# Fifteen-product groups: temporaries' sums moved between engines, weight splits and normalisation steps at other places

## The chip, the cores and the metric

The kernel runs on one core of a Trainium2 chip. The core has five engines that run side by side, each through its own queue in order: TensorE (PE in the profile; its weight loads are PEld), VectorE (DVE), ScalarE (ACT), GpSimd (POOL) and SyncE (SP), which here issues the DMAs. The metric is the device time of one execution in microseconds (us). Three runs of the kernel before took 1329.54, 1331.19 and 1333.52 us; the median is 1331.19 us.

## The reference

All arrays are float32. A pooled attention (2 batches, 8 heads, 1152 keys) gives 1152 tokens of 512 features. They go through a dense layer pair with the Mish function, and the result x through eight experts whose weights per token come from eight rounds of Sinkhorn normalisation:

```python
def _moe2_ref(x, w_gate, w1, w2):            # x 1152x512, w1 8x512x1024, w2 8x1024x512
    logits = x @ w_gate
    P = np.exp(logits - logits.max())
    for _ in range(8):
        P /= P.sum(1, keepdims=True) + 1e-09
        P /= P.sum(0, keepdims=True) + 1e-09
        P *= N / E
    out = 0
    for e in range(E):
        h = np.maximum(x @ w1[e], 0.0)
        out += P[:, e:e + 1] * (h @ w2[e])
    return out
```

Attention and Mish layers are untouched by the change; the experts are where it acts.

## The kernel before

**Arithmetic.** Every float32 operand is kept as two fp32r parts, high and low (`split_hi`, `split_lo`, lines 74 to 81). A product is three matmuls: high by low, low by high, high by high.

**The experts.** The 64 hidden chunks (8 experts by 8 chunks of 128) are worked through in order. The first four go the plain way (`expert_up`, and `down(-1, t)`), the other 60 in 20 groups of three (`groups`, g = 0 to 19). A group first computes its hidden values, 3 chunks by 3 token blocks of 384. Plainly that would be 9 block pairs by 2 halves of the features, 18 products; the kernel uses a scheme with 15 products of sums of blocks (`ORDER3`): sums of weights (`w_sum`), split into high and low (`w_split`), sums of tokens made once before (`x_prep`), and sums of the results afterwards (`after`). The program names a product by its number (9, 13, 3, 11, 12, 1, 2, 5, 10, 14, 7, 8, 0, 6, 4, in this order) and a result block by chunk and token block ("00" is chunk 0, token block 0). Each product is six matmuls of 384 columns (L983), so a product phase has 90.

**PSUM.** The nine result blocks of a group live in the eight PSUM banks: pool `ps_o` has three, `ps_h` five. Blocks 01, 10 and 22 come from `ps_o`, the other six from `ps_h` in the order 00, 12, 11, 02, 20, 21. Block 21, which product 7 (the eleventh) opens, therefore gets the bank of block 00 and has to wait until 00 has been read for the last time.

**Results.** ACT copies some results out of PSUM (`copy`, L1000) as temporaries t9, t13, t3, t11, u12, t1, t10, u14, u7. Six sums or differences of temporaries (`pair`, L1005) follow, two on POOL (s11 = t3 - t9 and u12 = u12 - t11), four on DVE. A block is finished (`fin`) by adding a temporary to the bank on DVE (L1014), the high part by a Relu on ACT (L1018) and the low part on DVE (L1019), which is issued after the L1014 of the next block to be finished. So 00 is released by this chain on DVE, in order: add 00 (needs u12), low part of 10, add 11 (needs s11), low part of 00.

**Down.** Then `down(g, t)` for nine tiles of 128 tokens: 9 matmuls of 512 columns each (L1142) into a `ps_o` bank, 81 in all. DVE adds the result, times the gate, to `oacc` (L1150). Five of the 20 groups hold chunks of two experts: there a tile has two segments with two banks and two L1150. In group 0 the gate is applied later, as POOL scales `oacc` (L1195).

**The order** on each engine is the order of the code; nothing is reordered. During the downs of a group `next_weights` makes the next group's eleven weight sums on DVE in steps k = 0 to 2 (L949) and splits the first eight (high part ACT, low part POOL) in steps 1 to 3. The other seven are split after products 0 to 6, and the second weights of the group (`down_split`, three chunks, both parts on POOL) after products 0, 2 and 4. The raw weights go through three SBUF buffers, `wraw`: two tiles of first and two of second weights a group, so a load waits for the last reader of the tile three places earlier.

**Sinkhorn.** `gate_steps` holds ten steps: `gate_max`, `gate_exp` (with the first row normalisation) and eight `sinkhorn_cols`. A column step is a small matmul over `csum` on PE and six short DVE instructions that end in the next `csum`. A step is taken at j = 0 and 2 of the remaining `expert_up`s, after tiles 4, 6 and 8 of `down(-1)`, and after products 2, 5, 8, 11 and 14 of group 0.

Of the kernel before, what the change touches and what calls it, by code (L numbers as in the profile page):

```python
# [23 lines left out]
def pool_attention_mish_sinkhorn_kernel(  # L24
# [790 lines left out]
    def sinkhorn_cols(it):  # L815
        ps = ps_h.tile([P, 512], F32, tag="h", name=f"psk{it}")
        nc.tensor.matmul(ps[:, 0:E], lhsT=ones, rhs=csum, start=True, stop=True)
        nc.vector.reciprocal(crec, ps[:, 0:E])
        nc.vector.scalar_tensor_tensor(
            out=Pv, in0=Pv, scalar=float(NT) / E, in1=crec.unsqueeze(1).to_broadcast([P, NTT, E]),  # L820
            op0=ALU.mult, op1=ALU.mult)
        if it + 1 < ROUNDS:
            sinkhorn_rows()
# [106 lines left out]
    def down_split(g, j):  # L930
        if g not in wdt:
            wdt[g] = tuple(wpools["d0"].tile([P, 4, GF], F32R, tag="wd" + x, name=f"wdb{x}{g}") for x in "hl")
        split_hi(nc.gpsimd, wdt[g][0][:, j, :], raws_d[g][j])
        split_lo(nc.gpsimd, wdt[g][1][:, j, :], raws_d[g][j], wdt[g][0][:, j, :])
# [10 lines left out]
    def w_sum(g, k):  # L945
        n, a, op, b = WSUM[k]
        inplace = {11: "10", 0: "21"}.get(n)
        out = w_get(g, inplace) if inplace else wsum.tile([P, HD, P], F32, tag=f"s{n}", name=f"s{n}_{g}")
        nc.vector.tensor_tensor(out=out, in0=w_get(g, a), in1=w_get(g, b), op=PLUS[op])  # L949
        ws[g, n] = out  # L950
# [71 lines left out]
    def after(g, n):  # L1022

        v, o = nc.vector, nc.gpsimd
# [5 lines left out]
        if n == 3:  # L1030
            copy(g, "t3", "10")
            pair(g, o, "s11", "t3", "-", "t9")
# [3 lines left out]
        if n == 12:  # L1036
            copy(g, "u12", "11")
            pair(g, o, "u12", "u12", "-", "t11")
# [64 lines left out]
    with tc.tile_pool(name="xt", bufs=3, side="right") as xt_p:  # L1103
        todo_x = list(range(len(XSUM)))
        for j, u in enumerate(ups):
            if j in (0, 2):
                gate_step()
            expert_up(NG1, *u)
            for _ in range(2 if j % 2 else 1):
                if todo_x:  # L1110
                    x_prep(todo_x.pop(0))
# [11 lines left out]
    wdt[-1] = w2t[NG1]  # L1123

    def down(g, t):
# [101 lines left out]
```

## Time and profile before

| | |
|---|---|
| runs, median (range) | 1331.19 us (1329.54 to 1333.52) |
| profiled execution | 1332.02 us, span in the trace 1329.8 us |
| PE busy, share of the span | 1239.2 us, 93% |
| DVE | 888.2 us, 67% |
| POOL | 700.4 us, 53% |
| ACT | 623.3 us, 47% |
| mean granted TensorE clock | 0.985 |

The span falls into attention (to about 350 us), the Mish layers (to about 480 us), the change to the experts with `down(-1)` (to 539.79 us) and the 20 groups (to the end). PE is busy nearly all the time, and its order is fixed, so the places to read are those where it waits: an instruction that stalls on PE delays everything behind it. Matmuls are pipelined: one of 384 columns is shown as 0.34 us, but the next starts about 0.174 us after it. A row with `[2.68 <-DVE hlall L1019]` says that the engine stood idle 2.68 us before this instruction, until DVE finished the instruction of line 1019 that writes `hlall`.

### The profile page before, as it was taken

The page shows a single profiled execution, that of the slowest core. Times are in us where ns is not written, and L with a number is a line of the kernel's source. Part 1 is how long each engine was busy: PE and PEld are TensorE (multiplying, and loading weights), DVE is VectorE, ACT ScalarE, POOL GpSimd, SP SyncE. Part 2 cuts the span into 40 slices and gives each one's busy share as a digit, 9 for nine tenths or more (in the row PEclk, how much of TensorE's full clock was granted, in tenths as well). Part 3 has the DMA queues.
Part 4 walks back from the last instruction along what each step waited for, and adds up shares of the span by engine and source line. Part 5 has one row for each costly group of instructions (what it writes and reads, how often), then busy time and mean ns, then how long its engine had stood idle before and what let it go on. Part 6 is the DMA issues. An engine that isn't in the chain of part 4 may idle for free.

```text
span 1329.8 us, 19342 instructions
## 1 busy us (share of the span) xinstructions
PE 1239.2 (93%) x6832; PEld 1133.4 (85%) x6832; DVE 888.2 (67%) x1726; ACT 623.3 (47%) x1432; POOL 700.4 (53%) x738
## 2 busy tenths in 40 slices
PE   8999999999999997898999998998999998999898
PEld 7999999999999996787788887877887876888687
DVE  7899999955443338667666666667656677766665
ACT  7899998875544434332233332323333332333231
POOL 7888888544343324383455444445455444554442
PEclk9999999999999999899999999999999999999999
DMA  4433332222222100110111110111111011111011
GB/s 116 101 92 92 92 96 70 71 83 83 89 82 78 40 17 8 40 35 22 48 48 40 48 48 16 41 48 48 41 48 32 25 48 48 41 48 48 21 35 71
DMA packets 55759, 73.15 MB, mean 55 GB/s; under 512 B 5744, under 2 KB 37872, under 8 KB 55664
## 3 DMA queue, kind: packets, MB, share of 16 engines
q1 hardware_dynamic: 55664, 71.93, 18.9%
q8 instruction: 54, 0.88, 0.3%
q14 instruction: 41, 0.34, 0.1%
HBM read 64.50 MB, written 2.36 MB: 50 GB/s over the span
## 4 chain that ended last, share of the span: by engine, by line
PE 68%; DVE 13%; POOL 11%; issue 5%; ACT 2%; DMA 0%; POOLq 0%; DVEq 0%; SPq 0%; ACTq 0%
PE po L1142 25%; PE c L983 9%; PE ph L219 8%; PE po L725 8%; PE psS L441 6%; PE psA L520 6%; PE psT L495 5%; POOL wslotsl L81 4%; DVE c L1014 2%; DVE s L949 2%; DVE hlall L1019 2%; POOL wdbl L81 2%; POOL wdbh L78 2%; DVE oacc L1150 2%; POOL sparel L1005 1%
## 5 line engine op out<-in xcount | busy, mean ns | idle before, releaser
L81 POOL TENSOR_TENSOR wslotsl<-s,wslotsh 128x256 fp32r<-128x256 f32 x180 | 140.6, 791 | 236.2 <-ACT wslotsh L74 236.1
L1142 PE MATMUL po<-wdbl,hhall 128*128 128x512 f32 (+1 forms) x543 | 217.0, 400 | 15.9 <-DVE oacc L1150 15.5
L1150 DVE SCALAR_TENSOR_TENSOR oacc<-po,Pm,oacc 128x512 f32<-128x512 f32 (+1 forms) x217 | 159.6, 745 | 86.6 <-PE po L1142 83.5
L1142 PE MATMUL po<-wdbh,hlall 128*128 128x512 f32 (+1 forms) x543 | 214.6, 395 | 0.0
L1142 PE MATMUL po<-wdbh,hhall 128*128 128x512 f32 (+1 forms) x543 | 214.5, 395 | 0.0
L1018 ACT ACTIVATE hhall<-c 128x384 fp32r<-128x384 f32 x180 | 88.6, 492 | 180.7 <-DVE c L1014 178.0
L81 POOL TENSOR_TENSOR wslotsl<-rawu,wslotsh 128x256 fp32r<-128x256 f32 x120 | 94.0, 799 | 134.6 <-ACT wslotsh L74 134.6
L1000 ACT ACTIVATE t<-c 128x384 f32<-128x384 f32 x80 | 39.2, 490 | 264.4 <-PE c L983 264.4
L1142 PEld LDWEIGHTS po<-wdbl,hhall 128*128 128x128 f32 x543 | 102.4, 189 | 47.4 <-DVE oacc L1150 24.0
L1142 PEld LDWEIGHTS po<-wdbh,hhall 128*128 128x128 f32 x543 | 102.4, 189 | 24.5
L1142 PEld LDWEIGHTS po<-wdbh,hlall 128*128 128x128 f32 x543 | 102.5, 189 | 22.7
L501 DVE TENSOR_TENSOR etl<-psT,eth 128x384 fp32r<-128x384 f32 (+1 forms) x240 | 112.1, 504 | 9.4 <-ACT eth L498 9.3
L466 POOL TENSOR_SCALAR e<-e,rc 128x1152 f32<-128x1152 f32 x72 | 89.4, 1242 | 43.5 <-DVE rc L465 15.7
L446 DVE TENSOR_SCALAR_CACHE_REDUCE sc<-psS 128x1152 f32<-128x1152 f32 x72 | 97.4, 1353 | 14.6 <-PE psS L441 13.6
L1019 DVE SCALAR_TENSOR_TENSOR hlall<-c,hhall 128x384 fp32r<-128x384 f32 x180 | 98.3, 546 | 2.0
L983 PE MATMUL c<-x2h,wslotsl 128*128 128x384 f32 x280 | 97.5, 348 | 0.0
L498 ACT ACTIVATE eth<-psT 128x384 fp32r<-128x384 f32 (+1 forms) x240 | 92.7, 482 | 8.8 <-PE psT L495 8.7
L983 PE MATMUL c<-x2l,wslotsh 128*128 128x384 f32 x280 | 96.6, 345 | 0.0
L983 PE MATMUL c<-x2h,wslotsh 128*128 128x384 f32 x280 | 96.4, 344 | 0.0
L1014 DVE TENSOR_TENSOR c<-c,t 128x384 f32<-128x384 f32 x80 | 44.8, 560 | 74.7 <-ACT t L1000 73.2
L454 ACT ACTIVATE e<-sc,nm 128x1152 f32<-128x1152 f32 x72 | 92.1, 1279 | 0.5 <-DVE sc L446 0.5
L495 PE MATMUL psT<-ident,e 128*128 128x128 f32 x648 | 85.6, 275 | 1.3 <-POOL e L466 0.8
(349 smaller groups left out, 3261.9 us busy)
## 6 DMA issues: line engine op xcount, KB each, us to landing
rawd<-in_moe_w_dram SPq DMA_DIRECT2D x60, 256.0 KB, 2.9
rawu<-in_moe_w_dram SPq DMA_DIRECT2D x30, 384.0 KB, 3.2
raw<-in_moe_w_in_dram SPq DMA_DIRECT2D x16, 512.0 KB, 3.8
raw<-in_moe_w_out_dram SPq DMA_DIRECT2D x16, 512.0 KB, 3.7
kraw<-in_k_dram SPq DMA_DIRECT2D x16, 288.0 KB, 3.2
vraw<-in_v_dram SPq DMA_DIRECT2D x16, 288.0 KB, 2.8
qraw<-in_q_dram SPq DMA_DIRECT2D x7, 576.0 KB, 4.3
qT<-qT SPq DMA_DIRECT2D x28, 128.0 KB, 2.5
```

The costliest lines, as they stand in the source:

```text
L81: eng.tensor_tensor(out=lo, in0=src, in1=hi.bitcast(F32), op=ALU.subtract)
L219: nc.tensor.matmul(ps[:, 0:TH], lhsT=a, rhs=b, start=(n == 0), stop=(n == len(ops) - 1))
L446: nc.vector.tensor_scalar(sc, ps[:, :, 0:TH], -1.0, None, op0=ALU.mult, op1=ALU.min, accum_out=nm)
L454: nc.scalar.activation(e, sc.rearrange("p a b -> p (a b)"), AF.Exp, bias=nm, scale=-1.0, accum_out=rs)
L495: nc.tensor.transpose(ps[:, i, :], e[:, c * P:(c + 1) * P], ident)
L498: nc.scalar.activation(eh[:, cs, o:o + b - a], ps[:, 0:3, a:b], AF.Copy)
L501: nc.vector.tensor_tensor(out=el[:, cs, o:o + b - a], in0=ps[:, 0:3, a:b], in1=eh[:, cs, o:o + b - a].bitcast(F32), op=ALU.subtract)
L725: nc.tensor.matmul(ps[:, 0:TH], lhsT=a, rhs=b, start=(n == 0), stop=(n == len(ops) - 1))
L983: nc.tensor.matmul(cb[c], lhsT=a_, rhs=b_, start=FIRST[n] and m == 0, stop=LAST[n] and m == len(ops) - 1, skip_group_check=True)
L1019: los.append(lambda: nc.vector.scalar_tensor_tensor(out=lo, in0=b, scalar=0.0, in1=hi.bitcast(F32), op0=ALU.max, op1=ALU.subtract))
L1142: nc.tensor.matmul(ps[:, 0:w], lhsT=a, rhs=b[:, c, cs], start=(n == 0), stop=(n == len(ops) - 1))
L1150: nc.vector.scalar_tensor_tensor(out=oa, in0=ps[:, 0:w], scalar=gate, in1=oa, op0=ALU.mult, op1=ALU.add)
```

## The change

Nothing is computed differently but for the order of some sums. Six things move:

1. s11 and u12 are computed on DVE (`v`) in place of POOL (`o`).
2. The three second-weight splits of a group: the first in step 7 of the downs before (in group 0 after product 0), the others after products 7 and 9 (were 0, 2, 4). The tile is one ring of four chunk places for all groups.
3. The weight sums are spread over steps 0 to 6 of the downs; sums 8, 10 and 14 are made on POOL.
4. In two-expert groups the second segment's bank comes from `ps_h`; the column sums of Sinkhorn come from `ps_o`.
5. The gate steps are taken later: `expert_up` j = 2 and 4, tiles 7 and 8 of `down(-1)`, products 3 and 5 of group 0, tiles 1, 3, 5 of its downs, product 3 of group 1.
6. The scaling of `oacc` moves from group 0 to group 1: products 10, 12, 14, then the down tiles, three ahead.

```diff
-        ps = ps_h.tile([P, 512], F32, tag="h", name=f"psk{it}")
+        ps = ps_o.tile([P, 512], F32, tag="o", name=f"psk{it}")
...
     def down_split(g, j):
-        if g not in wdt:
-            wdt[g] = tuple(wpools["d0"].tile([P, 4, GF], F32R, tag="wd" + x, name=f"wdb{x}{g}") for x in "hl")
-        split_hi(nc.gpsimd, wdt[g][0][:, j, :], raws_d[g][j])
-        split_lo(nc.gpsimd, wdt[g][1][:, j, :], raws_d[g][j], wdt[g][0][:, j, :])
+        if "all" not in wdt:
+            wdt["all"] = tuple(wpools["d0"].tile([P, 4, GF], F32R, tag="wd" + x, name=f"wdb{x}") for x in "hl")
+        wh, wl = wdt[g, j] = tuple(y[:, (CH * g + j) % 4, :] for y in wdt["all"])
+        split_hi(nc.gpsimd, wh, raws_d[g][j])
+        split_lo(nc.gpsimd, wl, raws_d[g][j], wh)
...
-            pair(g, o, "s11", "t3", "-", "t9")
+            pair(g, v, "s11", "t3", "-", "t9")
...
-            pair(g, o, "u12", "u12", "-", "t11")
+            pair(g, v, "u12", "u12", "-", "t11")
...
-            if j in (0, 2):
+            if j in (2, 4):
                 gate_step()
...
-                pl, tag = (ps_h, "h") if g < 0 and 3 <= t < 8 else (ps_o, "o")
+                pl, tag = (ps_h, "h") if (3 <= t < 8 if g < 0 else si) else (ps_o, "o")
...
-        for j in {0: range(0, 4), 1: range(4, 8), 2: range(8, 11)}.get(k, ()):
-            w_sum(g, j)
+        v, o = nc.vector, nc.gpsimd
+        for n, eng in {0: ((5, v), (8, o), (11, v)), 1: ((12, v), (2, v)), 2: ((10, o), (4, v)), 3: ((14, o),),
+                       4: ((0, v),), 5: ((7, v),), 6: ((6, v),)}.get(k, ()):
+            w_sum(g, n, eng)
...
+        if k == 7 and g > 0:
+            down_split(g, 0)
+
+    def scale(k):
+        nc.gpsimd.tensor_scalar(
+            oacc[:, TILES[k], :], oacc[:, TILES[k], :], Pm[:, TILES[k], 0:1], 0.0, op0=ALU.mult, op1=ALU.add)
...
-        if t in (4, 6, 8):
+        if t in (7, 8):
             gate_step()
...
-            if k in (0, 2, 4):
-                down_split(g, k // 2)
+            if k in ((0, 7, 9) if g == 0 else (7, 9)):
+                down_split(g, {0: 0, 7: 1, 9: 2}[k])
...
-            if g == 0 and k % 3 == 2:
+            if (g, k) in ((0, 3), (0, 5), (1, 3)):
                 gate_step()
+            if g == 1 and k in (10, 12, 14):
+                assert not gate_steps
+                scale(k // 2 - 5)
...
-            if g == 0:
-                assert not gate_steps
-                nc.gpsimd.tensor_scalar(
-                    oacc[:, t, :], oacc[:, t, :], Pm[:, t, 0:1], 0.0, op0=ALU.mult, op1=ALU.add)
+            if g == 0 and k in (1, 3, 5):
+                gate_step()
+            if g == 1 and k + 3 < NTT:
+                scale(k + 3)
```

First place: DVE in the product phase of group 5 (one expert), from its first instruction to the low part of block 00. Before (L1014 finishes a block, L1019 is a low part, L1005 a sum of temporaries):

```order
L1014 TENSOR_TENSOR c_5_8347<-c_5_8347,t_5_8369 128x384
L1014 TENSOR_TENSOR c_5_8375<-c_5_8375,t_5_8396 128x384
L1019 SCALAR_TENSOR_TENSOR hlall<-c_5_8347,hhall 128x384
L1005 TENSOR_TENSOR t_5_8369<-sparel,t_5_8369 128x384
L1014 TENSOR_TENSOR c_5_8362<-c_5_8362,spareh 128x384
L1019 SCALAR_TENSOR_TENSOR hlall<-c_5_8375,hhall 128x384
L1014 TENSOR_TENSOR c_5_8403<-c_5_8403,sparel 128x384
L1019 SCALAR_TENSOR_TENSOR hlall<-c_5_8362,hhall 128x384
```

The same stretch of the changed kernel, where these lines are 1016, 1021 and 1007:

```order
L1016 TENSOR_TENSOR c_5_8341<-c_5_8341,t_5_8359 128x384
L1007 TENSOR_TENSOR sparel<-t_5_8372,t_5_8348 128x384
L1016 TENSOR_TENSOR c_5_8365<-c_5_8365,t_5_8384 128x384
L1021 SCALAR_TENSOR_TENSOR hlall<-c_5_8341,hhall 128x384
L1007 TENSOR_TENSOR spareh<-spareh,t_5_8384 128x384
L1007 TENSOR_TENSOR t_5_8359<-sparel,t_5_8359 128x384
L1016 TENSOR_TENSOR c_5_8352<-c_5_8352,spareh 128x384
L1021 SCALAR_TENSOR_TENSOR hlall<-c_5_8365,hhall 128x384
L1016 TENSOR_TENSOR c_5_8391<-c_5_8391,sparel 128x384
L1021 SCALAR_TENSOR_TENSOR hlall<-c_5_8352,hhall 128x384
```

Two sums of temporaries, `sparel` (s11) and `spareh` (u12), now stand on DVE ahead of the addition to block 00 (the sixth row before, the seventh now).

Second place: POOL in the same product phase, from the low part of split 8. `wslotsl` are low parts of first weights, `wdbh` and `wdbl` the parts of the second weights. Before:

```order
L81 TENSOR_TENSOR wslotsl<-s_5_8238,wslotsh 128x256
L78 TENSOR_SCALAR wdbh_8358<-rawd_0_8298 128x512
L81 TENSOR_TENSOR wdbl_8359<-rawd_0_8298,wdbh_8358 128x512
L81 TENSOR_TENSOR wslotsl<-s_5_8240,wslotsh 128x256
L1005 TENSOR_TENSOR sparel<-t_5_8382,t_5_8354 128x384
L81 TENSOR_TENSOR wslotsl<-s_5_8262,wslotsh 128x256
L78 TENSOR_SCALAR wdbh_8358<-rawd_0_8298 128x512
L81 TENSOR_TENSOR wdbl_8359<-rawd_0_8298,wdbh_8358 128x512
L81 TENSOR_TENSOR wslotsl<-s_5_8220,wslotsh 128x256
L1005 TENSOR_TENSOR spareh<-spareh,t_5_8396 128x384
L81 TENSOR_TENSOR wslotsl<-rawu_1_8159,wslotsh 128x256
L78 TENSOR_SCALAR wdbh_8358<-rawd_1_8301 128x512
```

After, to the end of the phase:

```order
L81 TENSOR_TENSOR wslotsl<-s_5_8247,wslotsh 128x256
L81 TENSOR_TENSOR wslotsl<-s_5_8266,wslotsh 128x256
L81 TENSOR_TENSOR wslotsl<-s_5_8302,wslotsh 128x256
L81 TENSOR_TENSOR wslotsl<-s_5_8212,wslotsh 128x256
L81 TENSOR_TENSOR wslotsl<-rawu_1_8151,wslotsh 128x256
L81 TENSOR_TENSOR wslotsl<-s_5_8315,wslotsh 128x256
L81 TENSOR_TENSOR wslotsl<-s_5_8249,wslotsh 128x256
L78 TENSOR_SCALAR wdbh<-rawd_0_8286 128x512
L81 TENSOR_TENSOR wdbl<-rawd_0_8286,wdbh 128x512
L78 TENSOR_SCALAR wdbh<-rawd_1_8289 128x512
L81 TENSOR_TENSOR wdbl<-rawd_1_8289,wdbh 128x512
```

The seven low parts now follow each other, the two sums of temporaries are gone from POOL, and the last two second-weight splits (four instructions) stand behind the seventh low part.

Third place: DVE at the end of `down(-1)`, where the first column steps stand (`psk` is the column sum that PE made, `s` and `rawu` are weight sums of group 0). Before:

```order
L949 TENSOR_TENSOR s_0_6603<-rawu_1_6143 128x256
L949 TENSOR_TENSOR rawu_1_6143<-rawu_1_6143 128x2x128
L949 TENSOR_TENSOR s_0_6626<-rawu_0_6141,s_0_6603 128x256
L949 TENSOR_TENSOR s_0_6628<-rawu_0_6141,s_0_6626 128x256
L818 RECIPROCAL crec<-psk_6634 128x8
L819 SCALAR_TENSOR_TENSOR Pm<-Pm,crec 128x9x8
L808 TENSOR_REDUCE rsum<-Pm 128x9
L809 RECIPROCAL rsum<-rsum 128x9
L810 TENSOR_TENSOR Pm<-Pm,rsum 128x9x8
L812 TENSOR_REDUCE csum<-Pm 128x8
```

After:

```order
L951 TENSOR_TENSOR s_0_6621<-rawu_1_6143 128x256
L951 TENSOR_TENSOR rawu_1_6143<-rawu_1_6143 128x2x128
L951 TENSOR_TENSOR s_0_6683<-rawu_0_6141,s_0_6621 128x256
L818 RECIPROCAL crec<-psk_6685 128x8
L819 SCALAR_TENSOR_TENSOR Pm<-Pm,crec 128x9x8
L808 TENSOR_REDUCE rsum<-Pm 128x9
L809 RECIPROCAL rsum<-rsum 128x9
L810 TENSOR_TENSOR Pm<-Pm,rsum 128x9x8
L812 TENSOR_REDUCE csum<-Pm 128x8
L951 TENSOR_TENSOR s_0_6707<-rawu_0_6141,s_0_6683 128x256
```

The first column step stood behind all eleven weight sums; now it stands behind seven, with one sum after it.

## Rows read from the trace of the kernel before

**Rows 1.** Who waited for whom on PE, whole run: us in total, times, longest.

```profile
PE c L983 <- DVE hlall L1019: 52.3, 20, 2.7
...
PE po L1142 <- DVE oacc L1150: 15.5, 13, 2.2
...
PE psk L817 <- DVE csum L812: 9.2, 3, 7.1
...
PE psm L797 <- DVE mx L793: 1.3, 1, 1.3
```

**Rows 2.** PE around product 7 of group 5: start, duration, instruction, idle before.

```profile
749.68 0.34 PE L983 MATMUL c<-x14h,wslotsh 128*128 128x384 f32 x1
...
752.70 0.41 PE L983 MATMUL c<-x7h,wslotsl 128*128 128x384 f32 x1 [2.68 <-DVE hlall L1019]
```

**Rows 3.** Windows of group 5: product phase, downs; length, busy by engine, PEclk, DMA.

```profile
739.36:758.02 18.66, 15.98 (x91) 15.63 (x90) 9.83 (x19) 9.23 (x23) 12.83 (x15) 1.00 0.23 71
758.02:776.92 18.90, 18.90 (x83) 15.22 (x82) 14.61 (x24) 3.71 (x10) 6.58 (x8) 1.00 0.06 14
```

**Rows 4.** ACT in group 5's product phase: high part 11, copy of u12.

```profile
745.69 0.41 ACT L74 ACTIVATE wslotsh<-s 128x256 fp32r<-128x256 f32 x1
...
745.99 0.48 ACT L1000 ACTIVATE spareh<-c 128x384 f32<-128x384 f32 x1
```

**Rows 5.** DVE in group 5's product phase.

```profile
747.20 0.56 DVE L1005 TENSOR_TENSOR t<-sparel,t 128x384 f32<-128x384 f32 x1 [1.48 <-ACT sparel L1000]
...
750.60 0.57 DVE L1014 TENSOR_TENSOR c<-c,spareh 128x384 f32<-128x384 f32 x1 [2.85 <-POOL spareh L1005]
...
752.01 0.55 DVE L1019 SCALAR_TENSOR_TENSOR hlall<-c,hhall 128x384 fp32r<-128x384 f32 x1
...
753.98 1.03 DVE L1005 TENSOR_TENSOR t<-t,spareh 128x384 f32<-128x384 f32 x1
...
758.19 0.54 DVE L1019 SCALAR_TENSOR_TENSOR hlall<-c,hhall 128x384 fp32r<-128x384 f32 x1
```

**Rows 6.** POOL in group 5's product phase.

```profile
742.22 0.62 POOL L78 TENSOR_SCALAR wdbh<-rawd 128x512 fp32r<-128x512 f32 x1
...
742.92 1.30 POOL L81 TENSOR_TENSOR wdbl<-rawd,wdbh 128x512 fp32r<-128x512 f32 x1
...
747.27 1.64 POOL L81 TENSOR_TENSOR wdbl<-rawd,wdbh 128x512 fp32r<-128x512 f32 x1
...
748.87 0.74 POOL L81 TENSOR_TENSOR wslotsl<-s,wslotsh 128x256 fp32r<-128x256 f32 x1
```

**Rows 7.** POOL before the groups, and late in the downs of group 5.

```profile
517.06 1.84 POOL L81 TENSOR_TENSOR x2l<-xt,x2h 128x768 fp32r<-128x768 f32 x1 [2.02 <-ACT x2h L74]
...
761.52 0.92 POOL L81 TENSOR_TENSOR wslotsl<-rawu,wslotsh 128x256 fp32r<-128x256 f32 x1
```

**Rows 8.** DVE at the same places.

```profile
515.09 0.95 DVE L889 TENSOR_TENSOR xt<-acc 128x768 f32<-128x768 f32 x1
...
517.29 2.42 DVE L889 TENSOR_TENSOR xt<-acc 128x768 f32<-128x768 f32 x1
...
760.99 0.85 DVE L949 TENSOR_TENSOR s<-rawu 128x256 f32<-128x256 f32 x1
```

**Rows 9.** Five two-expert down phases: sum of the five windows.

```profile
sum 117.11, PE 101.25 PEld 75.59 DVE 101.18 ACT 18.54 POOL 30.83; mean PE 20.25 PEld 15.12 DVE 20.24 ACT 3.71 POOL 6.17
```

**Rows 10.** Five product phases at a lower clock: the first, and the sum.

```profile
625.24:645.41 20.17, 17.49 (x92) 17.15 (x90) 10.64 (x20) 9.54 (x24) 12.83 (x15) 0.92 0.22 65
...
sum 100.74, PE 87.38 PEld 85.69 DVE 53.51 ACT 47.75 POOL 64.10; mean PE 17.48 PEld 17.14 DVE 10.70 ACT 9.55 POOL 12.82
```

**Rows 11.** Windows of `down(-1)` and of group 0's product phase.

```profile
504.15:539.79 35.64, 28.53 (x116) 22.78 (x115) 24.15 (x38) 13.89 (x27) 13.15 (x11) 0.86 0.03 8
539.79:564.15 24.36, 20.47 (x103) 19.47 (x102) 18.40 (x47) 9.84 (x24) 12.76 (x15) 0.86 0.18 55
```

**Rows 12.** Window of one column step on DVE.

```profile
531.84:533.45 1.61, 1.43 (x6) 0.50 0.00 0
```

More of the change, by code (lines that the diff above doesn't have):

```diff
@@ L943, in w_get, with w_sum @@
         return raws_u[g][int(z[1])][:, :, int(z[0]) * P:(int(z[0]) + 1) * P] if isinstance(z, str) else ws[g, z]
-    def w_sum(g, k):
-        n, a, op, b = WSUM[k]
+    def w_sum(g, n, eng):
+        _, a, op, b = next(x for x in WSUM if x[0] == n)
         inplace = {11: "10", 0: "21"}.get(n)
         out = w_get(g, inplace) if inplace else wsum.tile([P, HD, P], F32, tag=f"s{n}", name=f"s{n}_{g}")
-        nc.vector.tensor_tensor(out=out, in0=w_get(g, a), in1=w_get(g, b), op=PLUS[op])
+        eng.tensor_tensor(out=out, in0=w_get(g, a), in1=w_get(g, b), op=PLUS[op])
         ws[g, n] = out
@@ L1022, in after @@
     def after(g, n):
-        v, o = nc.vector, nc.gpsimd
+        v = nc.vector
         if n == 9:
@@ L1122, in pool_attention_mish_sinkhorn_kernel @@
     TILES = [0, 1, 2, 6, 7, 8, 3, 4, 5]
-    wdt[-1] = w2t[NG1]
+    for j in range(NFC):
+        wdt[-1, j] = tuple(y[:, j, :] for y in w2t[NG1])
     def down(g, t):
@@ L1129, in down @@
         w = DM // parts
-        whi, wlo = wdt[g]
-        for e, sl in segments(g):
+        for si, (e, sl) in enumerate(segments(g)):
             gate = Pm[:, t, e:e + 1]
             for j in range(parts):
-                pl, tag = (ps_h, "h") if g < 0 and 3 <= t < 8 else (ps_o, "o")
+                pl, tag = (ps_h, "h") if (3 <= t < 8 if g < 0 else si) else (ps_o, "o")
                 ps = pl.tile([P, 512], F32, tag=tag, name=f"po{g}_{t}_{e}_{j}")
@@ L1139, in down @@
                     hh, hl = hidden(c, t * P, (t + 1) * P)
-                    ops += [(hh, wlo, c), (hl, whi, c), (hh, whi, c)]
-                for n, (a, b, c) in enumerate(ops):
+                    whi, wlo = wdt[g, c]
+                    ops += [(hh, wlo), (hl, whi), (hh, whi)]
+                for n, (a, b) in enumerate(ops):
                     nc.tensor.matmul(
-                        ps[:, 0:w], lhsT=a, rhs=b[:, c, cs], start=(n == 0), stop=(n == len(ops) - 1))
+                        ps[:, 0:w], lhsT=a, rhs=b[:, cs], start=(n == 0), stop=(n == len(ops) - 1))
                 oa = oacc[:, t, cs]
```

## The prediction

> **What bounds the kernel now.** First the busy shares: TensorE is busy 93% of the span, so only its idle time, its clock and its own work can move the end, and the change leaves its matmuls alone. Then the list of who waited for whom on TensorE [rows 1]. The reader is to see one wait that comes 20 times, 2.7 us at most and 52.3 us in all: a product waiting for the low part of a block, once in each group. Behind it stand 15.5 us of downs waiting for the additions to `oacc`, 9.2 us of Sinkhorn matmuls waiting for `csum`, and 1.3 us for `mx`.
>
> The waiting matmul is the first of product 7, the eleventh product, whose bank is that of block 00 [rows 2]. It starts at 752.70 us; the one in front started at 749.68, and matmuls of a product are 0.175 us apart (59 steps from 739.36 to 749.68), so 2.85 us are lost. Without it the 90 matmuls take 15.7 us and not 18.66; the 81 of the downs take 18.90 and wait for nothing in group 5 [rows 3]. A group of one expert takes 37.56 us, of which 34.6 are TensorE's own.
>
> What does product 7 wait for? Its releaser is the low part of 00 at 752.01 on VectorE [rows 5], and that chain began late: the addition to 00 at 750.60 had waited 2.85 us for POOL, for u12. The copy of u12 was there at 745.99 + 0.48 [rows 4]. POOL came to it only after low parts of weights and a second-weight split whose low part alone took 1.64 us [rows 6]. So POOL's queue sets the loss, and VectorE was idle for it.
>
> Two more losses hang on waits. The five down phases of two-expert groups take 117.11 us [rows 9] where five single ones would take 94.5: 22.6 us, with VectorE busy 101.18 of them. And five product phases take 100.74 us where 93.3 would be usual; there the granted clock is 0.92, between 1.2 and 2.4 GHz, against 1.00 in group 5 [rows 3, 10]. That is 7.4 us, after TensorE had stood idle.
>
> **Part one: the two sums on VectorE.** I count from the start of a group (739.36 = 0). POOL no longer does s11, u12 and the early second-weight splits, so the low parts follow their high parts at once. u12's copy is at 6.63; VectorE can begin the difference at 7.2, as a copy takes 0.48 us. A sum of temporaries takes 0.56 us clean [rows 5] and frees the engine for the next about 0.47 after its start, as additions and low parts do. If all three sums (s11, u12, t13) were clean, the addition to 00 would stand at 8.3, the low part of 00 three instructions later at 9.7, and product 7, released 0.69 us after the start of that low part (752.01 to 752.70), at 10.4. Its place is 10.45 (60 by 0.174). The wait would be gone.
>
> But they are not clean. A VectorE instruction with both inputs in SBUF stops while POOL works: one of 0.95 us takes 2.42, from 517.29 to 519.71, beside a POOL instruction from 517.06 to 518.90, and ends 0.8 us behind its end [rows 7, 8]. POOL stops likewise: the low part issued at 761.52 ends at 762.44, 0.60 behind the VectorE sum (760.99 to 761.84), and 1.64 is a 1.30 behind such a sum [rows 6 to 8]. They take turns. The sum of t3 shows the price for this shape, 1.03 in place of 0.56 [rows 5]. Additions, low parts and `oacc` read one input from PSUM, and no such stretching shows in theirs.
>
> Where do they meet? High part 11 is at 6.33 [rows 4], its low part on POOL from 6.87 to 7.61 (0.41 for the high part, a hand-over, then 0.74 [rows 6]). u12 begins at 7.2 inside it and ends 0.42 behind it, at 8.03. Low part 12 then runs to 8.63; t13, waiting since 7.95, ends at 9.05. So the addition to 00 stands at 8.96, the low part of 00 at 10.37, product 7 at 11.06: a wait of 0.6 us remains of 2.85.
>
> **Part two: the second weights behind the low parts.** With relu 00 at 9.56 and high part 14 behind it, low part 14 ends near 11.2, and POOL goes straight on: high part of chunk 1 (0.62) to 11.8, low part (1.30) to 13.15, then chunk 2 [rows 6]. VectorE meets each with a sum. t3, ready at 12.36, ends at 13.55; the high part of chunk 2 runs to 14.07, u14 ends at 14.5; the low part of chunk 2 runs to 15.64, u7 ends at 16.06. Clean, u7 would end near 13.95. The six instructions from there to the low part of block 20 stand 0.47 us apart, so it is at 18.3. Now the downs begin at 15.7 + 0.6 = 16.3, and the eighth matmul of the first tile reads that low part: it wants to go at 17.9 and goes at 19.0. In the kernel before the low part at 758.19 was in time for the downs at 758.02 [rows 3, 5]. So 1.1 us is the new wait, at the head of the downs.
>
> No row shows a temporaries' sum behind a 1.30 us POOL instruction, so the price is bounded: from nothing (0.56 as t13 has it now [rows 5], no wait left) to POOL's whole remaining instruction, as laid out, 1.7 us a group. The 0.47 of the t3 row for each of u12, t13, t3, u14 and u7 would leave about 1.0. I take the upper end, since in every row the stopped instruction ends a fixed time behind the other's end. The Trainium skill has a rule for this, "SBUF — State Buffer", section "SBUF: two separate sides": whichever of a VectorE instruction with two SBUF inputs and a GpSimd instruction starts first keeps the shared ports for the whole instruction, and the other is blocked. By it the result is about 1268 us, by the clean 0.56 about 1234; the stretched rows agree with the rule.
>
> A one-expert group then takes 34.58 + 0.6 + 1.1 = 36.26 us, 1.30 less. For 18 groups (2 to 19) that is 23.4 us.
>
> **Part three: downs of two experts.** Eight banks in place of three let TensorE run about three tiles ahead, and eight sums in place of eleven stay on VectorE. Its work there is 18 additions (0.75 apart, 13.5 us) and eight sums of 0.42 to 0.85 [rows 8], so 17 to 20 us, beginning at 20.4 behind the last low part, against TensorE's 18.9 [rows 3]. Laid tile by tile, the addition that frees a bank is at least half a microsecond early. I take the waits as gone: 22.6, less 0.6 for group 1, where additions also wait for the moved scaling on POOL: 22.0. If VectorE stays the bound, half of it is lost. The weight sums on POOL (not in the trace; the low parts of the same size, 0.74 to 0.92 [rows 6, 7], are the nearest, and 0 to 1.8 each the bound) lie beside downs, where POOL works 6.6 of 18.9 us [rows 3], and cost nothing. If that cover fails, the first product of the next group waits. Loads move too: the second tile of first weights waits for the split at 13.2 (before 9.6) and is wanted near 21; nothing is queued behind it that is wanted sooner.
>
> **Part four: clock.** With no 2.85 us pause, and no pauses in the downs before it, I take the 7.4 us as gone; 0 to 7.4 is the bound.
>
> **Part five: Sinkhorn.** `down(-1)` takes 35.64 us for 108 matmuls worth 25.2 [rows 3, 11]: 10.4 lost, 7.1 of it waiting for `csum` behind eleven sums on VectorE, the rest at a lower clock and in small matmuls. Now VectorE, free of the token sums near 521, has seven sums (0.42 to 0.85) in front of the first column step of 1.61 us [rows 8, 12]; it ends at about 529, when TensorE, 1.3 us earlier for the missing `mx` wait, asks for it at 528.1. I take 1 to 1.5 us of wait: 10.0 gained, bounds 5 and 11.7. Group 0's products (24.36 [rows 11]) keep two column steps of five; each puts 1.6 us on VectorE ahead of block 00: 2.2 gained, bounds -2 and 7. Three steps in the downs of group 0 and their `ps_o` banks cost 1.5, the one in group 1 costs 0.3 more than it saves there.
>
> **The sum.** 23.4 + 22.0 + 7.4 + 10.0 + 2.2 - 1.5 - 0.3 = 63.2 us. The profiled execution took 1332.02 (2.2 outside its span), so 1268.8; it lies 0.8 above the median of the runs, so **1268**.
>
> **Rivals.**
> - *No collisions on the path.* If the sums slip between POOL's instructions, 1.7 us in each of 20 groups go as well: 1268 - 34 = 1234. For it: t13 is clean today though POOL splits beside it [rows 5, 6]. Against it: POOL's instructions now stand without gaps exactly where the sums fall.
> - *VectorE sets the pace.* If the delays grow (two-expert downs end late, t13 and t3 meet longer instructions), groups stay at 37.5 and the lower clock stays: 1268 + 23.4 + 7.4 = 1299. For it: VectorE's share of two-expert downs, 86%. Against it: three sums less there.
> - *The change does not do what it says:* u12 still late, as the copy and not POOL was the last link. Then only downs and Sinkhorn gain, also near 1300. Against it: the copy was there 4.1 us before the addition.
> - *Slower.* Each group now has two short pauses. If they kept the clock down in every group, a mean of 0.92 costs 1.5 us a group [rows 10], 30 in all, still faster; it decides from 3.2 us a group, a mean near 0.83, and at 0.80 (3.8 us, 75 in all) gives 1343. Against it: group 5 paused 2.85 us and ran at 1.00 [rows 3].
>
> **The numbers.** Forecast 55% (own range 1254 to 1284), no collisions 22%, VectorE's pace 17%, not as it says 4%, slower 2%. The range 1236 to 1294 holds the forecast and the near halves of both neighbours. About 0.3%, 4 us, is what a measurement can tell from no change: faster 0.96, within it 0.02, slower 0.02.
>
> **What would show it.** The list of waits of the changed kernel: the wait of product 7 near 0.6 us a group in place of 2.7, and a wait near 1 us of the first down for `hlall`. The sums of temporaries on VectorE: means near 1 us for u12, t13, t3 and u14, more for u7. POOL: no L1005 form, second-weight splits back to back. The two-expert downs at 19 us, PEclk 1.00 from group 2 on. The prediction is wrong if the sums stay at 0.56, if the first down waits for nothing, or if the two-expert downs still take over 21 us.

## The result and the profile after

The changed kernel takes 1261.36 us (1261.23 to 1261.57) against 1332.20 us, a ratio of 0.9471 [0.9454, 0.9487]. The forecast was 1268.0 us, with a range of 1236 to 1294. The granted clock is 1.00 over the whole span of 1259.6 us.

The busy shares of the changed kernel:

```profile
PE 1230.0 (98%) x6832; PEld 1120.1 (89%) x6832; DVE 921.0 (73%) x1706; ACT 622.0 (49%) x1432; POOL 727.3 (58%) x758
```

Who waited for whom on PE, changed kernel (total us, times, longest):

```profile
PE c L985 <- DVE hlall L1021: 6.2, 19, 0.3
PE po L1145 <- DVE hlall L1021: 5.7, 19, 0.3
...
PE psk L817 <- DVE csum L812: 1.2, 2, 0.9
...
PE po L1145 <- DVE oacc L1151: 0.2, 1, 0.2
```

Of [rows 1], 52.3 us for the low part in product 7 have become 6.2; the additions to `oacc` ask 0.2 and no longer 15.5; `csum` 1.2 and no longer 9.2. New is the second line: the downs wait 19 times for a low part.

The windows of the changed kernel: `down(-1)`, then products and downs in turn of groups 0, 1 and 2, a one-expert group from 713.93, and the downs of a two-expert group from 874.88:

```profile
503.39:528.93 25.54, 25.54 (x114) 20.64 (x113) 19.50 (x30) 12.97 (x27) 14.34 (x14) 1.00 0.00 1
528.93:547.21 18.28, 16.98 (x97) 16.07 (x96) 14.72 (x35) 8.96 (x22) 12.50 (x14) 1.00 0.19 59
547.21:569.31 22.10, 20.48 (x89) 15.80 (x88) 19.21 (x43) 4.76 (x12) 10.05 (x13) 1.00 0.11 36
569.31:586.38 17.07, 16.18 (x94) 15.89 (x92) 12.32 (x21) 9.04 (x22) 11.64 (x13) 1.00 0.19 51
586.38:605.47 19.09, 19.09 (x83) 15.14 (x82) 18.02 (x31) 4.15 (x11) 15.20 (x21) 1.00 0.07 25
...
713.93:730.23 16.30, 15.98 (x91) 15.61 (x90) 11.73 (x17) 8.25 (x21) 11.01 (x12) 1.00 0.16 48
...
730.23:750.06 19.83, 19.40 (x82) 15.14 (x82) 14.47 (x25) 4.65 (x12) 9.74 (x13) 1.00 0.12 40
...
874.88:894.73 19.85, 19.41 (x83) 15.14 (x82) 18.89 (x32) 4.64 (x12) 9.58 (x13) 1.00 0.09 27
```

The first four columns to read are start and end, length, PE and, after PEld, DVE; the third from the end is the clock. A product phase has gone from 18.66 to 16.30 us, the downs of one expert from 18.90 up to 19.83 [rows 3], those of two experts from a mean of 23.4 [rows 9] down to the same 19.85. `down(-1)` fell from 35.64 to 25.54 and group 0's products from 24.36 to 18.28 [rows 11], while group 0's downs take 22.10.

PE in the group that starts at 713.93, answering to [rows 2]:

```profile
724.25 0.34 PE L985 MATMUL c<-x14h,wslotsh 128*128 128x384 f32 x1
724.91 0.41 PE L985 MATMUL c<-x7h,wslotsl 128*128 128x384 f32 x1 [0.32 <-DVE hlall L1021]
...
730.23 0.39 PE L1145 MATMUL po<-wdbl,hhall 128*128 128x512 f32 x1
...
732.69 0.50 PE L1145 MATMUL po<-wdbh,hlall 128*128 128x512 f32 x1 [0.29 <-DVE hlall L1021]
```

Product 7 starts 0.66 us behind its forerunner, not 0.175: 0.49 lost. The eighth down matmul, due at 731.86 (seven steps of 0.233 behind 730.23), starts at 732.69: 0.83 lost. The idle time in brackets is smaller, since the record of the matmul in front reaches beyond the start that the next could have had; the loss is read from starts and from windows.

VectorE in the same group, answering to [rows 5]:

```profile
721.08 0.81 DVE L1007 TENSOR_TENSOR spareh<-spareh,t 128x384 f32<-128x384 f32 x1 [0.79 <-ACT spareh L1002]
721.81 1.09 DVE L1007 TENSOR_TENSOR t<-sparel,t 128x384 f32<-128x384 f32 x1
...
724.22 0.54 DVE L1021 SCALAR_TENSOR_TENSOR hlall<-c,hhall 128x384 fp32r<-128x384 f32 x1
...
726.18 1.21 DVE L1007 TENSOR_TENSOR t<-t,spareh 128x384 f32<-128x384 f32 x1
727.31 0.96 DVE L1007 TENSOR_TENSOR sparel<-sparel 128x384 f32<-128x384 f32 x1
728.20 1.65 DVE L1007 TENSOR_TENSOR spareh<-spareh,t 128x384 f32<-128x384 f32 x1
...
732.10 0.54 DVE L1021 SCALAR_TENSOR_TENSOR hlall<-c,hhall 128x384 fp32r<-128x384 f32 x1
```

And POOL, answering to [rows 6]:

```profile
721.43 1.05 POOL L81 TENSOR_TENSOR wslotsl<-rawu,wslotsh 128x256 fp32r<-128x256 f32 x1
...
725.68 1.29 POOL L81 TENSOR_TENSOR wdbl<-rawd,wdbh 128x512 fp32r<-128x512 f32 x1
726.95 0.92 POOL L78 TENSOR_SCALAR wdbh<-rawd 128x512 fp32r<-128x512 f32 x1
727.95 1.48 POOL L81 TENSOR_TENSOR wdbl<-rawd,wdbh 128x512 fp32r<-128x512 f32 x1
```

Read the two beside each other. The sum at 726.18 ends at 727.39, 0.42 behind the POOL low part that ended at 726.97. The one at 728.20 ends at 729.85, 0.42 behind the low part that ended at 729.43. POOL in turn took 0.92 us for a high part that is 0.62 clean [rows 6]. They take turns, as laid out, and the low part of block 20 comes 18.17 us after the group's start (732.10 - 713.93); 18.3 had been forecast.

### The profile page after: what moved, and what is told of

Its sections match the earlier page's. It is cut to its first block, busy times and chain, and to the rows that moved or that the text cites. A ratio compares the mean times of both kernels' runs of the same rounds, so it can differ in the third digit from the quotient of the medians.

```text
span 1259.6 us, 19402 instructions
## 1 busy us (share of the span) xinstructions
PE 1230.0 (98%) x6832; PEld 1120.1 (89%) x6832; DVE 921.0 (73%) x1706; ACT 622.0 (49%) x1432; POOL 727.3 (58%) x758
## 4 chain that ended last, share of the span: by engine, by line
PE 31%; DVE 13%; issue 6%; ACT 5%
PE po L1145 27%; DVE c L1016 6%; PE c L985 4%; DVE hlall L1021 3%; DVE t L1007 2%; DVE sparel L1007 2%; ACT hhall L1020 1%; ACT t L1002 1%; ACT spareh L1002 1%; ACT wslotsh L74 1%; DVE s L951 0%; DVE spareh L1007 0%; DVE oacc L1151 0%; DVE Pm L810 0%; DVE Pm L819 0%
## 5 line engine op out<-in xcount | busy, mean ns | idle before, releaser
L81 POOL TENSOR_TENSOR wslotsl<-s,wslotsh 128x256 fp32r<-128x256 f32 x180 | 143.4, 806 | 221.2 <-ACT wslotsh L74 221.1
L81 POOL TENSOR_TENSOR wslotsl<-rawu,wslotsh 128x256 fp32r<-128x256 f32 x120 | 97.0, 822 | 68.6 <-ACT wslotsh L74 68.6
L1145 PEld LDWEIGHTS po<-wdbh,hhall 128*128 128x128 f32 x543 | 102.0, 188 | 23.4
L466 POOL TENSOR_SCALAR e<-e,rc 128x1152 f32<-128x1152 f32 x72 | 89.0, 1236 | 43.7 <-DVE rc L465 16.7
L985 PE MATMUL c<-x2h,wslotsl 128*128 128x384 f32 x280 | 94.4, 337 | 0.0
L985 PE MATMUL c<-x2l,wslotsh 128*128 128x384 f32 x280 | 94.0, 336 | 0.0
L166 POOL TENSOR_TENSOR wt<-wt,raw 128x512 int32<-128x512 int32 x32 | 42.1, 1317 | 75.6 <-DVE wt L160 71.0
```

Of the source, the lines that this page charges most:

```text
L81: eng.tensor_tensor(out=lo, in0=src, in1=hi.bitcast(F32), op=ALU.subtract)
L466: nc.gpsimd.tensor_scalar(e, e, rc, 0.0, op0=ALU.mult, op1=ALU.add)
L985: nc.tensor.matmul(cb[c], lhsT=a_, rhs=b_, start=FIRST[n] and m == 0, stop=LAST[n] and m == len(ops) - 1, skip_group_check=True)
L1145: nc.tensor.matmul(ps[:, 0:w], lhsT=a, rhs=b[:, cs], start=(n == 0), stop=(n == len(ops) - 1))
```

## The experiments

Ratios are to the kernel before; each time is a median of four runs. An experiment undoes or adds its edit with all others in place, unless it says otherwise.

**The sums back on POOL.** The second-weight splits stay late.

```diff
-            pair(g, v, "s11", "t3", "-", "t9")
+            pair(g, nc.gpsimd, "s11", "t3", "-", "t9")
-            pair(g, v, "u12", "u12", "-", "t11")
+            pair(g, nc.gpsimd, "u12", "u12", "-", "t11")
```

> The changed kernel with s11 and u12 back on POOL, everything else as changed. My theory: what released product 7 was the emptied POOL queue, not the engine of the two sums. POOL, without the early second-weight splits, reaches u12 at about 7.6 of the group and ends it at 8.6, t13 on VectorE meets it and ends near 9.0, the low part of 00 stands near 10.3: the same 0.5 to 0.7 us of wait as in the changed kernel (10.29 there). About 1261 us, 1255 to 1268. Rival (moving the two sums to VectorE is what pays): the 2.85 us wait comes back, 2 us or more a group, 1300 us or more.

Measured: 1262.28 us, 0.9457 [0.9426, 0.9487]; products of groups 2 to 19 take 16.22 to 16.28 us, downs 19.79 to 19.86 up to group 18. Group 5's products:

```profile
716.33:732.61 16.28, 16.00 (x92) 15.66 (x90) 10.32 (x16) 8.24 (x21) 12.37 (x14) 1.00 0.16 48
```

Moving the sums to VectorE earns nothing once POOL's queue is free of the splits.

**The splits early again.** The sums stay on VectorE.

```diff
-            if k in ((0, 7, 9) if g == 0 else (7, 9)):
-                down_split(g, {0: 0, 7: 1, 9: 2}[k])
+            if k in (0, 2, 4):
+                down_split(g, k // 2)
...
-        if k == 7 and g > 0:
-            down_split(g, 0)
```

> The changed kernel with the three second-weight splits of a group after products 0, 2 and 4 again, s11 and u12 staying on VectorE. My theory: u12 no longer queues behind POOL, only collides with its instructions, so product 7 waits about 0.9 us, and the collisions at t3, u14 and u7 shrink (POOL does low parts of first weights there), so the first down waits little: 35.5 to 36.3 us a group, 1248 to 1264 us. Rival (the place of the splits is what pays): u12 and the chain late again, 37 us a group or more, 1280 us or more. With the run of the sums on POOL: if both stay below 1270, either half alone removes most of the wait.

Measured: 1255.24 us, 0.9406 [0.9370, 0.9442]: with the splits where they were, the kernel is faster than with the whole change. Group 5, products and downs:

```profile
712.52:729.08 16.56, 15.95 (x91) 15.61 (x90) 11.80 (x19) 8.66 (x22) 12.85 (x14) 1.00 0.25 80
729.08:748.36 19.28, 19.16 (x83) 15.16 (x82) 13.51 (x24) 4.23 (x12) 7.61 (x10) 1.00 0.05 14
```

Either edit alone takes away most of product 7's wait: the phase takes 16.56 us here, 16.3 with the late splits alone or with both edits, 15.7 without a wait. The late splits gain under 0.3 us there and cost the downs their head (19.28 us here, 19.83 with them late). Both edits undone with the rest of the change in place was not run; the kernel before (18.66) has to stand for it. The list of waits puts what is left at product 7 down to POOL:

```profile
PE c L985 <- POOL wdbh L78: 11.1, 18, 0.6
```

But a product reads no second weights. In group 5 the low part of 00 and product 7 stand thus:

```profile
723.07 0.54 DVE L1021 SCALAR_TENSOR_TENSOR hlall<-c,hhall 128x384 fp32r<-128x384 f32 x1
723.76 0.41 PE L985 MATMUL c<-x7h,wslotsl 128*128 128x384 f32 x1 [0.61 <-POOL wdbh L78]
```

Product 7 starts 0.69 us behind the start of that low part, as in the kernel before (752.01 to 752.70 [rows 2, 5]) and in the changed one (724.22 to 724.91). So it most likely waits for the same chain on VectorE, and a split on POOL that ends at the same moment is named in its place.

**One split earlier.** The second chunk is split after product 0, the third still after product 9.

```diff
-            if k in ((0, 7, 9) if g == 0 else (7, 9)):
-                down_split(g, {0: 0, 7: 1, 9: 2}[k])
+            for j in ({0: (0, 1), 9: (2,)} if g == 0 else {0: (1,), 9: (2,)}).get(k, ()):
+                down_split(g, j)
```

> The changed kernel with the second chunk's second-weight split after product 0 (was 7), the third still after product 9. My theory: POOL then has one split of 1.9 us behind its seventh low part and not two; t3 still meets it, u14 and u7 are clean, so the low part of block 20 is about 1.2 us earlier and the first down waits for nothing; product 7 waits as before, 0.6 us. About 35.2 us a group, 1243 to 1250 us. Rival (the wait of the first down is not from POOL's splits): 1261 us.

Measured: 1242.82 us, 0.9313 [0.9283, 0.9342], 0.2 us under the expected range. Products stay at 16.3, the downs are back at 18.89. So the wait at their head is the row of splits beside t3, u14 and u7, and half of that row is enough to be rid of it.

**Sums that read one side from PSUM.** All six sums take one operand straight from its bank; the copies of u12, u14 and u7, made only for them, go.

```diff
+    def pairp(g, out, x, op, y):
+        ...
+        get = lambda z: tmp[z] if z in tmp and z not in cb else cb[z]
+        nc.vector.tensor_tensor(out=tmp[out], in0=get(x), in1=get(y), op=PLUS[op])
...
-            pair(g, v, "s11", "t3", "-", "t9")
+            pairp(g, "s11", "10", "-", "t9")
-            copy(g, "u12", "11")
-            pair(g, v, "u12", "u12", "-", "t11")
+            pairp(g, "u12", "11", "-", "t11")
-            pair(g, v, "t13", "t1", "+", "t13")
+            pairp(g, "t13", "22", "+", "t13")
...
```

> The changed kernel, but each of the six sums of temporaries takes one operand straight from its PSUM bank in place of the SBUF copy (s11 from 10, u12 from 11, t13 from 22, t3 from 02, u14 from 20, u7 from 21); the copies of u12, u14 and u7 on ACT go. VectorE has the same instructions and POOL the same queue. My theory (the remaining 0.6 and 1.1 us a group come of VectorE and POOL stopping each other when both inputs are in SBUF): the six sums are 0.55 to 0.6 us each, product 7 and the first down wait for nothing, a group takes 34.7 to 35.0 us, 1233 to 1243 us. Rival (VectorE's own number of instructions in a row sets the remaining waits): the time stays at 1255 to 1262 us.

Measured: 1231.28 us, 0.9226 [0.9197, 0.9255]: the fastest kernel of the study. Its windows, the downs and products of one-expert groups and the downs of a two-expert one:

```profile
687.95:706.85 18.90, 18.90 (x83) 15.24 (x82) 12.13 (x20) 3.42 (x10) 9.59 (x12) 1.00 0.11 37
706.85:722.59 15.74, 15.74 (x92) 15.74 (x91) 11.08 (x22) 8.33 (x21) 9.53 (x12) 1.00 0.18 56
757.22:776.12 18.90, 18.90 (x83) 15.23 (x83) 17.46 (x29) 3.42 (x10) 9.35 (x12) 1.00 0.10 33
```

PE is busy in all of each phase. The sums there, and, for comparison, those of the changed kernel (count, busy us and mean ns):

```profile
L1013 DVE TENSOR_TENSOR spareh<-c,t 128x384 f32<-128x384 f32 x40 | 21.9, 548 | 0.0
L1013 DVE TENSOR_TENSOR t<-c,t 128x384 f32<-128x384 f32 x20 | 11.2, 558 | 12.4 <-ACT sparel L1002 12.4
L1013 DVE TENSOR_TENSOR t<-t,c 128x384 f32<-128x384 f32 x20 | 10.9, 544 | 0.0
```

```profile
L1007 DVE TENSOR_TENSOR spareh<-spareh,t 128x384 f32<-128x384 f32 x40 | 49.3, 1232 | 14.6 <-ACT spareh L1002 14.6
L1007 DVE TENSOR_TENSOR t<-t,spareh 128x384 f32<-128x384 f32 x20 | 24.2, 1210 | 0.0
L1007 DVE TENSOR_TENSOR t<-sparel,t 128x384 f32<-128x384 f32 x20 | 20.8, 1041 | 0.4 <-ACT sparel L1002 0.4
L1007 DVE TENSOR_TENSOR sparel<-t,t 128x384 f32<-128x384 f32 x20 | 16.1, 806 | 24.8 <-ACT t L1002 24.8
```

0.55 us against 0.81 to 1.23, with POOL's instructions the same. In a one-expert group the two waits are worth (16.30 - 15.74) + (19.83 - 18.90) = 1.49 us. The medians are 30.1 us apart: groups 2 to 19 carry 27.4 of them, and nearly all the rest is in group 0's downs (19.54 against 22.10). The three copies that go shorten u12's and u7's chains too; s11, t13 and t3 keep their copies and are as short as the rest.

**The same on the kernel before.** Here two things move at once: the six sums read PSUM, and s11 and u12 go from POOL to VectorE. Nothing else of the change is in it.

```diff
-            pair(g, o, "s11", "t3", "-", "t9")
+            pairp(g, "s11", "10", "-", "t9")
...
```

> The kernel before with one edit: all six sums of temporaries on VectorE with one operand from the PSUM bank (as in the run where the sums read PSUM), second-weight splits, weight sums, banks and Sinkhorn steps as before. My theory: the chain to the low part of 00 no longer meets POOL at all, a product phase takes 15.7 to 16 us, the last low part comes early enough for the packed weight sums in one-expert downs (34.6 to 35 us a group), while two-expert downs (23.4 us) and the start of group 0 stay as before: 1266 to 1280 us. Rival (the downs then run into the packed sums, as in the run with packed sums, 1.5 us a group): 1290 to 1300 us.

Measured: 1266.62 us, 0.9511 [0.9488, 0.9535]. Working over the six sums alone saves 65 us, nearly as much as the whole change, though `csum` still waits 7.1 us at its longest and two-expert downs still take 22.5 to 24.1. Nearly all of it lies in the product phases: 59.9 us in groups 2 to 19. How much belongs to reading PSUM and how much to taking two sums off POOL was not separated on this kernel. In the run with early splits the sums stood on VectorE with both inputs in SBUF, and the phase took 16.56 us, against 18.66 before and 15.74 here. If the other edits don't matter in that phase, most of the gain belongs to the move. A two-expert down phase, the products behind it, and the down phase of the same kind in group 9:

```profile
774.37:796.91 22.54, 20.21 (x83) 14.74 (x82) 19.78 (x32) 3.44 (x10) 6.18 (x8) 1.00 0.04 13
796.91:812.65 15.74, 15.74 (x92) 15.74 (x91) 11.34 (x23) 8.35 (x21) 10.61 (x13) 1.00 0.29 84
881.91:905.99 24.08, 20.97 (x82) 16.23 (x82) 19.90 (x32) 3.44 (x10) 6.16 (x8) 0.93 0.04 12
```

All product phases of groups 1 to 19 run at a clock of 1.00 here, where the kernel before had 0.92 in five of them [rows 10]; with product 7's wait gone, that loss is gone. But the clock can fall without that wait: within the downs of groups 9 and 17, the two longest of the five two-expert ones (24.1 us), it is 0.93, and TensorE had paused only for additions there. The loss stands in the downs then, and is part of their length.

**Three banks.** The second segment's bank comes from `ps_o` again.

```diff
-                pl, tag = (ps_h, "h") if (3 <= t < 8 if g < 0 else si) else (ps_o, "o")
+                pl, tag = (ps_h, "h") if g < 0 and 3 <= t < 8 else (ps_o, "o")
```

> The changed kernel with the second expert's segment in the three ps_o banks again. My theory: in two-expert groups VectorE begins its additions about 4 us behind the start of the downs, and with three banks, two to a tile, TensorE can be only one tile ahead, so it waits about 3 us in each of five groups: 1276 us, 1268 to 1285. Rival (fewer and spread weight sums on VectorE are enough): 1262 us. Second rival (the banks are the whole gain there): 4.5 us a group and the lower clock again, 1288 us.

Measured: 1272.13 us, 0.9525 [0.9485, 0.9565]. Only two-expert downs grow, to between 21.55 and 22.10 us; single ones of groups 2 to 18 stay at 19.83 to 19.86.

**Weight sums packed.** All eleven on VectorE in steps 0 to 2, as before.

```diff
-        for n, eng in {0: ((5, v), (8, o), (11, v)), 1: ((12, v), (2, v)), 2: ((10, o), (4, v)), 3: ((14, o),),
-                       4: ((0, v),), 5: ((7, v),), 6: ((6, v),)}.get(k, ()):
+        for n, eng in {0: ((5, v), (8, v), (11, v), (12, v)), 1: ((2, v), (10, v), (14, v), (4, v)),
+                       2: ((0, v), (7, v), (6, v))}.get(k, ()):
```

> The changed kernel with all eleven weight sums on VectorE in steps 0 to 2 again; the second segment stays in ps_h. My theory: in one-expert groups the third addition ends about when the sixth tile wants its bank, 0 to 0.3 us lost; in two-expert groups about 1 us late: 1262 to 1274 us, 1268 likeliest. Rival (the banks alone carry the two-expert downs): 1261 us. Second rival (the sums' place is the gain): 1280 us or more.

Measured: 1297.05 us, 0.9712 [0.9678, 0.9747]. The forecast was wrong by over 20 us, and the rival with the high price was right: the edit is worth 35.7 us. It does two things, since the sums 8, 10 and 14 also come back from POOL to VectorE; which of the two costs more was not separated. Most of the loss lies where I had seen no wait at all, in one-expert downs: 21.42 us here, 19.83 in the changed kernel. In two-expert downs it is 22.0 against 19.85. A one-expert down phase, and the new line on top of the list of waits:

```profile
741.47:762.89 21.42, 19.93 (x83) 15.00 (x82) 17.55 (x28) 4.75 (x12) 8.81 (x10) 1.00 0.13 37
```

```profile
PE po L1145 <- DVE oacc L1153: 21.9, 36, 1.1
```

VectorE near the end of a one-expert group's sums, and POOL beside it:

```profile
752.51 0.74 DVE L1153 SCALAR_TENSOR_TENSOR oacc<-po,Pm,oacc 128x512 f32<-128x512 f32 x1
753.51 2.26 DVE L951 TENSOR_TENSOR s<-rawu,s 128x256 f32<-128x256 f32 x2
755.69 2.06 DVE L1153 SCALAR_TENSOR_TENSOR oacc<-po,Pm,oacc 128x512 f32<-128x512 f32 x3
```

```profile
753.16 0.90 POOL L78 TENSOR_SCALAR wdbh<-rawd 128x512 fp32r<-128x512 f32 x1
754.15 1.34 POOL L81 TENSOR_TENSOR wdbl<-rawd,wdbh 128x512 fp32r<-128x512 f32 x1
```

Two sums of this form, 0.44 us on the mean in the changed kernel, take 2.26 us together, in turns with the split that the change itself put into the downs. The three additions to `oacc` behind them come in one row, and the banks that they free are wanted earlier. PE in the same stretch:

```profile
756.49 0.50 PE L1145 MATMUL po<-wdbl,hhall 128*128 128x512 f32 x1 [0.81 <-DVE oacc L1153]
```

**Banks and sums together.** Both of the last two edits.

> Both of the last two edits at once: three banks and packed sums, the rest as changed. My theory: VectorE's work in a two-expert down phase (20.2 us before) again starts late and cannot be run ahead of: 4.5 us or more lost in each of five groups, and the lower clock behind some of them, 1284 to 1298 us. If the two edits are independent the losses of the two runs add up; if each alone costs nothing and both cost 20 us, either of them is cover enough.

Measured: 1313.86 us, 0.9840 [0.9805, 0.9875]: again too low a forecast. Apart they cost 10.8 and 35.7 us, together 52.5. One-expert downs are at 21.4 to 21.6 us and two-expert ones at 24.7 to 26.1. The lower clock came, though within the downs and not behind them: it is 0.93 in three of the five two-expert phases (25.6 to 26.1 us), and 1.00 in all products. What is left of the change, with three banks and packed sums, saves about 19 us of 70.

**Packed sums on the version with PSUM operands.** This asks whether the place of the sums matters only because VectorE is late.

> The changed kernel with sums reading PSUM and the weight sums packed on VectorE in steps 0 to 2. My theory: packing cost 36 us because VectorE began its additions 3.9 us behind the start of the downs; with the sums reading PSUM it begins about 2 us earlier against TensorE, so packing costs 0 to 0.5 us in a one-expert group and 1 to 2 in a two-expert one: 1231 to 1246 us. Rival (the number of sums on VectorE in the downs is the cost, whenever it begins): 1260 us or more.

Measured: 1246.74 us, 0.9361 [0.9342, 0.9381], 0.7 us above the range. Packing costs 15.5 us here and 35.7 there; in one-expert downs 0.45 us (19.34 against 18.90), in two-expert ones 1.0 to 1.3, in group 0's downs 4.3. So more than half of its price goes when the sums read PSUM and the downs begin without a late VectorE; the rest is what packing costs with the split that stands in the downs in both kernels. So the place of the sums matters most, but not only, because VectorE is late.

**Gate steps as before.** The Sinkhorn steps at their old places, `csum` in `ps_h`, the scaling in group 0.

```diff
-        if t in (7, 8):
+        if t in (4, 6, 8):
...
-            if (g, k) in ((0, 3), (0, 5), (1, 3)):
+            if g == 0 and k % 3 == 2:
                 gate_step()
...
```

> The changed kernel with the Sinkhorn steps, their bank pool and the scaling of oacc where they were. My theory: the first column steps stand in front of the end of the first downs again and VectorE reaches them late, so most of the 10.9 us by which group 0 now starts earlier is lost, and group 0 has five steps in its products and none in its downs, which costs 3 to 5 us there and gives 4 back: 1268 to 1275 us. Rival (the earlier start comes of the fewer weight sums on VectorE, not of the later steps): 1261 to 1264 us.

Measured: 1271.41 us, 0.9522 [0.9488, 0.9556]; groups 2 to 19 are the same, and the wait for `csum` is back, 5.8 us in all and 4.2 at its longest. `down(-1)` takes 32.56 us, 7.0 more than in the changed kernel.

## Why the prediction was nearly right, and where not

The mechanism and the term that carries most held. Point by point, forecast and then measured:

- *Wait of product 7 left:* 0.6 us a group; 0.56 (16.30 against the 15.74 that this phase takes without a wait). *New wait at the head of the downs:* 1.1; 0.93. *A one-expert group:* 36.26; 36.13 (16.30 + 19.83). The upper end that I chose for the stretched sums, turn by turn, was the right one: u12, t13, t3 and u7 take 0.81, 1.09, 1.21 and 1.65 us. The rule that the Trainium skill states in "SBUF — State Buffer", section "SBUF: two separate sides", agrees with these rows: each of these sums ends 0.40 to 0.42 us behind the POOL instruction that stood in its way. The experiment with operands from PSUM shows the other side: there the sums take 0.55 us beside the same instructions.
- *Two-expert downs:* waits gone; they are, 19.83 to 19.86 us. *Clock:* 1.00; it is.
- *Sinkhorn as a whole:* 10.0 + 2.2 - 1.5 - 0.3 = 10.4 us; undoing it costs 10.1. Its parts were sized less well: kept as before, group 0's products take 23.13 us and not 18.28, so 4.9 was gained there and not 2.2; group 0's downs 18.97 and not 22.10, so they pay 3.1 and not 1.5; group 1's products pay 0.8 (16.31, 17.07) and not 0.3. The term of 10.0 is the whole gain of `down(-1)` (35.64 to 25.54), but undoing the steps gives back only 7.0 of it, and a start 0.7 us later; the other edits gave the rest. So that the totals agree, 10.4 and 10.1, is partly luck.

The forecast was 6.6 us too high, and the step that failed is "For 18 groups (2 to 19) that is 23.4 us". The wait stands 20 times in [rows 1]. For groups 0 and 1 I priced only the Sinkhorn steps and forgot product 7's wait, which goes there too: with the steps as before, group 0's products fall to 23.13 from 24.36 and group 1's to 16.31 from 18.6. Products of group 0 came out at 18.28 where I had 22.2, those of group 1 at 17.07 where I had 18.9, together 5.7 us. The rest: groups 2 to 19 are 1.7 better in all (651.0, where 18 of 36.26 make 652.7), `down(-1)` ends 0.9 earlier (528.93 against 529.8), group 1's downs are 0.4 better (19.09, where I had 18.9 + 0.6) and group 0's 1.6 worse. That sums to 7.1 us; the sum stood for a span of 1268.8 - 2.2 = 1266.6 us, 7.0 above the measured 1259.6.

Two of my reasons were right in number and wrong in what they credited. I gave the gain at product 7 to "the two sums on VectorE"; on POOL they give the same (1262.28 us), since late splits are enough to empty POOL's queue. And I valued the spread of the weight sums only in two-expert downs. The gain at the head of each group would have been lost in its downs without it: 21.42 us in place of 19.83. My own rival "VectorE sets the pace", 1299 us, is near what the kernel with packed sums does (1297), in part by chance: a group takes 37.7 us there, as that rival had it, but the granted clock is 0.999, and the rival counted 7.4 us for a lower one. It comes through VectorE's late start in the downs, which I had laid out and had not carried on into the additions behind it.

The prediction had put 34 us on the collisions, in its rival without them, and did not ask how to be rid of them: taking one operand from PSUM gives 30 us back. What stays open is how the 30 divide between shorter sums and the three dropped copies.

## What to carry to other kernels

When a VectorE operation with two SBUF inputs stands beside GpSimd work, look first for an operand that still lies in PSUM: here that was worth 30 us on top of the change. On the kernel before, together with taking two sums off GpSimd, it was worth 65 us, where the whole change of six parts gave 71. When a wait at the head of a stage is removed, lay the next stage out again from the new start, for work that was in nobody's way may now be what ends last. And to credit one of several edits, undo it with the others in place: here two edits each did most of the same job, and two others cost 6 us more together than the sum of each alone.

## What the runs showed of the hardware

One operand in PSUM was enough to end the mutual stops: the sums had been expected at 0.55 to 0.6 us and took 0.55. VectorE in the version with PSUM operands, and POOL beside it:

```profile
718.13 0.55 DVE L1013 TENSOR_TENSOR t<-t,c 128x384 f32<-128x384 f32 x1
718.59 0.55 DVE L1013 TENSOR_TENSOR sparel<-sparel,c 128x384 f32<-128x384 f32 x1
719.05 0.55 DVE L1013 TENSOR_TENSOR spareh<-c,t 128x384 f32<-128x384 f32 x1
```

```profile
717.64 1.31 POOL L81 TENSOR_TENSOR wdbl<-rawd,wdbh 128x512 fp32r<-128x512 f32 x1
718.91 0.63 POOL L78 TENSOR_SCALAR wdbh<-rawd 128x512 fp32r<-128x512 f32 x1
```

The three sums and the two POOL instructions overlap in time and each takes its clean duration; in the changed kernel the same three sums took 1.21, 0.96 and 1.65 us and the same POOL instructions 1.29 and 0.92. Over the whole run the high parts of second weights on POOL fall from a mean of 0.73 us to 0.62 and their low parts from 1.37 to 1.30, so both engines gain.
